# Pooling batch 0 in skewed steps, copying the transposed w1 once, and a new order of the main loop

## The chip, the cores and the metric

The kernel runs on one core of one Trainium2 chip. The time is that of one execution on the device in microseconds (us); the result compares medians of several executions. One further execution is recorded by the hardware profiler, and all lines of a profile come from that one. TensorE (PE) has a row for its matmuls and one for its weight loads (PEld, which overlap the matmuls); VectorE is DVE, ScalarE ACT, GpSimd POOL, SyncE SP.

## The reference

Two operations follow each other. The first is attention over a set of 32 inducing points, in both directions, on four batches of 12,544 tokens of 128 channels:

```python
scale = 1.0 / np.sqrt(C)
def mab(q, kv):
    s = scale * (q @ kv.transpose(0, 2, 1))
    s = s - s.max(-1, keepdims=True)
    a = np.exp(s)
    a /= a.sum(-1, keepdims=True) + 1e-09
    return a @ kv
h = mab(I, x)          # 32 pooled vectors per batch
y = mab(x, h)          # every token attends to the 32
```

The second is a maxout layer on the 50,176 rows of y, with 1,024 hidden units:

```python
g = np.maximum(y @ w1, y @ w2)
out = g @ w_out        # float32
```

## The kernel before

All matmuls run in float16. A chunk is 128 tokens; a batch has 98 chunks.

**Algebra.** The maximum is written as y w1 plus relu(y (w2 - w1)). As y is a mix of the 32 rows of h with the weights e, the kernel forms hwd = h (w2 - w1) and m1 = h (w1 w_out) once for each batch. A token's output is then relu(e hwd) w_out + e m1, divided by the sum of e at the end.

**Pooling of batch 0** stands ahead of everything else. x comes in eleven parts of 14 down to 3 chunks, loaded by POOL's queue; the first comes through SP and is cast on the chip. Each part is transposed on TensorE (`p1_transpose`; first half copied out by VectorE, second by ScalarE), gives scores against the inducing points, of which ScalarE takes the exponential (`p1_scores`), and is accumulated into h and the sums (`p1_accum`). A few matmuls on constant data (`fill`) keep TensorE busy in the first parts. Then h is scaled and copied (`small_h`), w1, which VectorE has negated in place, is transposed on TensorE into w1T (`weights_2`), the sums are turned into reciprocals rs and rw by VectorE (`small_sums`), and hwd comes in quarters and a half (`small_hwd`). w1T with w_out gives w1out (`weights_3`), which `small_m1` needs.

**The main loop** handles blocks of up to four quarters of up to four chunks. `stage` computes the scores of a block's tokens against h in four column tiles of the array; ScalarE takes the exponential into e2. A row phase (`phase`, the matmuls of L978) runs up to four jobs in four row tiles: a job is either 512 columns of e hwd, whose relu is taken by ScalarE (L994) or VectorE (L997), or the start of an output group with e m1. Final matmuls (L801) multiply relu by w_out into the group's bank; VectorE multiplies by the reciprocal of the sum of e (L828), and SP stores the result. Each of the eight PSUM banks is held by one job until ScalarE or VectorE has read it. `keep_busy` adds stopgap matmuls (L758) where a wait is foreseen.

**Pooling of batches 1 to 3** runs inside the main loop in six units of 16 chunks each: x is transposed by DMAs on SP's queue (L171, fourteen for a batch), `pool_scores` (L308) computes the scores of a unit in column tiles, ScalarE takes the exponential into one of five buffers eu (L319), SP transposes that by a DMA into eT (L345), and `pool_accum` (L364) accumulates two units at a time. Unit 5 takes over the buffer of unit 0. `small_rep`, `small_h`, `small_hwd` and `small_m1` follow.

**The order** is made while the kernel is built. A `Clock` adds up assumed durations for TensorE, ScalarE and VectorE and keeps for each bank the time at which it comes free. At each step the loop picks side work, a column job, a row phase or a final matmul by these times and by due dates counted in finished chunks (`at`). A pool score may be placed once the x transposes it needs were placed 8 us ago on that clock; for unit 5 it asks that the transpose of unit 0's exponential has been placed, not that it is over. The table `DEV` alters the choice at some steps: 1 prefers a final matmul, 2 a phase, 3 passes over column work, 4 allows it early. On the chip every engine then follows its own fixed list, waiting on semaphores.

Of the kernel before, what the change touches and what calls it, by code (L numbers as in the profile page):

```python
# [9 lines left out]
F16 = mybir.dt.float16  # L10
# [92 lines left out]
def kernel(  # L103
# [38 lines left out]
    def bank(shape, dtype=F32, only=None):  # L142
        i = min(range(8), key=lambda j: ck.bank[j]) if only is None else only
        uid[0] += 1
        return i, psum.tile(shape, dtype, name=f"ps{uid[0]}", tag=f"bank{i}", bufs=1)
# [51 lines left out]
    with tc.manual_schedule(engines={ET.PE, ET.DVE, ET.Activation, ET.Pool, ET.SP}):  # L197
# [63 lines left out]
        def p1_accum(b, i, lo=0, hi=P1):  # L261
            k0, n = parts[b][i]
            et, ready = st[b]["et", i]
            hi = min(hi, n)
            xn = xn_at[b, i]
            if b == 0:
                last = i == len(parts[0]) - 1
                ck.wait(ready, "p1")
                for j in range(lo, hi, 4):
                    m = min(4, hi - j)  # L270
                    nc.tensor.matmul(  # L271
                        out=st[0]["eps"][0 : m * M, 0:1],
                        lhsT=et[:, j : j + m, :].rearrange("p k m -> p (k m)"),
                        rhs=ones16[:, 0:1],
                        start=(i == 0 and j == 0),
                        stop=(last and j + m == n),
                        skip_group_check=True,
                    )
                for j in range(lo, hi):
                    nc.tensor.matmul(  # L280
                        out=st[0]["hps"][:, 0:M],
                        lhsT=xn[:, j, :],
                        rhs=et[:, j, :],
                        start=(i == 0 and j == 0),
                        stop=(last and j == n - 1),
                    )
                st[0]["end"] = ck.run(0.029 * (hi - lo) + 0.03 * ((hi - lo + 3) // 4))
                return
# [156 lines left out]
        def small_sums(es, ready):  # L445

            ps = st[0]["eps"]
            ck.wait(ready, "p1")
            nc.tensor.matmul(out=ps[:, 2:3], lhsT=rep32, rhs=es, start=True, stop=True, skip_group_check=True)
            end = ck.run(0.11)  # L450
            st[0]["rs"] = smp.tile([128, 1], F32, name="rs_0", tag="rs_")
            st[0]["rw"] = smp.tile([128, 1], F32, name="rw_0", tag="rw_")
            nc.vector.reciprocal(out=st[0]["rs"], in_=ps[:, 2:3])
            nc.vector.tensor_scalar(out=st[0]["rw"], in0=st[0]["rs"], scalar1=1.0 / scale, scalar2=None, op0=ALU.mult)
            ck.bank[st[0]["eb"]] = st[0]["rsr"] = ck.on_dve(end, 0.34)

        def small_hwd(b, halves=(0, 1)):
            if 0 in halves:
                st[b]["hwd"] = smp.tile([128, J], F16, name=f"hwd_{b}", tag="hwd")
            hwd = st[b]["hwd"]  # L460
            for half in halves:
                for n in range(2 if b == 0 and half == 0 else 1):
                    w = 256 if b == 0 and half == 0 else 512
                    bi, ps = bank([128, 512])
                    ps = ps[:, 0:w]
                    sl = slice(512 * half + w * n, 512 * half + w * (n + 1))
                    ck.wait(max(ck.bank[bi], st[b]["hT4r"]), "p1")
                    if b == 0:
                        nc.tensor.matmul(out=ps, lhsT=st[b]["hT4"], rhs=w2h[:, sl], start=True, stop=False)
                        nc.tensor.matmul(out=ps, lhsT=st[b]["hT4"], rhs=w1h[:, sl], start=False, stop=True)  # L470
                        end = ck.run(0.43 * w / 512)
                    else:
                        nc.tensor.matmul(out=ps, lhsT=st[b]["hT4"], rhs=w21[:, sl], start=True, stop=True)  # L473
                        end = ck.run(0.215)
                    if half == 0 and n == 0:
                        if b == 0:
                            nc.vector.tensor_scalar(
                                out=hwd[:, sl], in0=ps, scalar1=st[0]["rw"], scalar2=None, op0=ALU.mult
                            )
                        else:  # L480
                            nc.vector.tensor_copy(out=hwd[:, sl], in_=ps)
                        ck.bank[bi] = ck.on_dve(end, 0.07 + w / 970.0)
                    else:
                        nc.scalar.activation(
                            out=hwd[:, sl], in_=ps, func=AF.Copy, scale=st[0]["rw"] if b == 0 else 1.0
                        )
                        ck.bank[bi] = ck.on_act(end, 0.06 + w / 1200.0)
                    st[b]["hwdr"] = max(ck.bank[bi], st[b].get("hwdr", 0.0))
# [33 lines left out]
                nc.gpsimd.tensor_sub(w21[:, 512 * h : 512 * (h + 1)], w_of[h][0], w_of[h][1])  # L522

        def weights_2():
            for g in range(2):
                bi, ps = bank([128, 4, 128], F16)
                ck.wait(ck.bank[bi], "w")
                for j in range(4):
                    jb = 4 * g + j
                    nc.tensor.transpose(ps[:, j, :], w1h[:, 128 * jb : 128 * (jb + 1)], identity16)  # L530
                end = ck.run(0.056 * 4)
                if g == 0:
                    nc.vector.tensor_copy(out=w1T[:, 0:4, :], in_=ps)
                    ck.bank[bi] = ck.on_dve(end, 0.4)
                else:
                    nc.scalar.copy(out=w1T[:, 4:8, :], in_=ps)
                    ck.bank[bi] = w_of["w1T"] = ck.on_act(end, 0.5)

        def weights_3():
            bi, ps = bank([128, 512])  # L540
# [105 lines left out]
        def fill(n):  # L646
            bi, ps = bank([128, 512])
            for _ in range(n):
                nc.tensor.matmul(out=ps, lhsT=warm[:, 0:128], rhs=warm, start=True, stop=True)  # L649
            ck.run(0.22 * n)  # L650
# [7 lines left out]
        for n in ("h", "e"):  # L658
            st[0][n + "b"], st[0][n + "ps"] = bank([128, 512])
            ck.bank[st[0][n + "b"]] = INF  # L660
        for i in range(4):
            p1_transpose(0, i, 2 if i == 0 else 0)
            if i < 3:
                fill(2 - i // 2)
            if i == 0:
                bi, ps = bank([128, 512])
                nc.tensor.transpose(ps[:, 0:M], ind_sb, identity32[0:M, 0:M])
                nc.vector.tensor_copy(out=inducingT, in_=ps[:, 0:M])
                ck.bank[bi] = 0.0
                nc.vector.reduce_sum(out=diag, in_=identity32.rearrange("p (k m) -> p m k", m=M), axis=AX.X)  # L670
                for dst, f in ((rep32, DOWN / scale), (repd, 1.0)):
                    nc.vector.tensor_scalar(
                        out=dst.rearrange("p (k m) -> p k m", m=M),
                        in0=diag[:, None, :].broadcast_to((128, 4, M)),
                        scalar1=f,
                        scalar2=None,
                        op0=ALU.mult,
                    )
            if i > 0:
                p1_accum(0, i - 1)  # L680
            p1_scores(0, i)
        last = len(parts[0]) - 1
        p1_transpose(0, 4)
        p1_accum(0, 3)
        p1_transpose(0, 5)
        p1_scores(0, 4)
        for i in range(6, last + 1):
            p1_transpose(0, i)
            p1_scores(0, i - 1)
            p1_accum(0, i - 2)  # L690
        p1_scores(0, last)
        p1_accum(0, last - 1)
        p1_accum(0, last)
# [4 lines left out]
        sums = small_h(0)  # L698
        weights_2()
        small_sums(*sums)  # L700
        stage(blocks[0])
        small_hwd(0, (0,))
        blocks[0].staged = max(blocks[0].staged, st[0]["hwdr"])
# [174 lines left out]
        def want_linear():  # L878
# [12 lines left out]


        DEV = {
            31: 1, 54: 1, 107: 2, 141: 1, 148: 1, 177: 4, 201: 1, 231: 1, 268: 1, 285: 1, 289: 1, 297: 2,
            308: 3, 310: 4, 331: 1, 339: 4, 357: 4, 358: 4, 366: 1, 375: 1, 397: 1, 409: 1, 446: 3, 457: 1,
            463: 4, 465: 3, 488: 1, 518: 2, 542: 3, 567: 4, 612: 3, 653: 1, 752: 1, 805: 1, 810: 2, 829: 1,
            834: 4, 842: 1, 846: 1, 863: 1, 900: 1, 920: 4, 946: 1, 950: 1, 966: 1, 1005: 1, 1025: 1, 1050:
            2, 1111: 1, 1119: 1, 1138: 1, 1152: 1, 1163: 1, 1190: 1, 1201: 1, 1282: 1, 1294: 1, 1299: 1,
            1301: 4, 1349: 4, 1362: 3, 1363: 2, 1370: 4, 1379: 1, 1396: 2, 1435: 1, 1459: 1, 1469: 1, 1472:
            3, 1519: 1, 1534: 1, 1536: 3, 1543: 4, 1572: 3, 1606: 1, 1617: 4, 1635: 1, 1654: 3, 1686: 1,  # L900
            1701: 3, 1729: 1
        }
        LIMIT = -16

# [288 lines left out]
```

The softmax here doesn't subtract the row's maximum and nothing guards it: scores larger than these inputs give would overflow.

## Time and profile before

| what | value |
|---|---|
| median of 4 executions | 328.05 us (327.6 to 328.36) |
| the profiled execution | 327.6 us, of which its span 325.5 us |
| TensorE matmul, busy | 320.2 us, 98% |
| weight loads | 242.4 us, 74% |
| VectorE, busy | 282.4 us, 87% |
| ScalarE, busy | 281.8 us, 87% |
| GpSimd, busy | 25.4 us, 8% |
| final matmuls | 3,136 |
| relus on ScalarE and on VectorE | 465 of 605 ns, 319 of 682 ns |
| DMA | 53.65 MB, 165 GB/s in the mean |

The span runs from the first instruction of the program to the last; the profiled execution's time has some 2.1 us around it. A matmul's duration includes its way through the array, so the 220 ns of a final matmul are no measure of how fast they follow one another; starts are. A line of the timeline has start, length over all its instructions, engine, source line, operation, output and input, shape, count, and in brackets the idle time ahead of it with what ended it. In the list of waits and in the groups, an arrow names what an engine waited for.

### The profile page before, as it was taken

How to read it: one execution, taken by the hardware profiler on the slowest of the kernel's cores; microseconds unless marked ns; L12 is line 12 of the kernel's file. 1: busy time of each engine (PE TensorE's matmuls, PEld its weight loads, DVE VectorE, ACT ScalarE, POOL GpSimd, SP SyncE). 2: the span in 40 equal slices, each digit the busy share in tenths (PEclk: the TensorE clock that was granted, in tenths of full speed). 3: DMA queues.
4: the chain of work that ended last, by engine and by line, in shares of the span. 5: the costliest groups of instructions: out<-in, count | busy, mean ns of one | idle time of the engine just before them, and what ended most of it. 6: DMA issues, size and time to landing. Idle time of an engine off the chain costs nothing.

```text
span 325.5 us, 12587 instructions
## 1 busy us (share of the span) xinstructions
PE 320.2 (98%) x5404; PEld 242.4 (74%) x5404; DVE 282.4 (87%) x518; ACT 281.8 (87%) x564; POOL 25.4 (8%) x51
## 2 busy tenths in 40 slices
PE   7999999999999999999999999999999999999995
PEld 3886777777777777777777777777777777777785
DVE  3359998998989999999989989898999999989873
ACT  3689899999978999999988999899979999999961
POOL 7352030000040000000040000000000000000000
PEclk9999999999999999999999999999999999999999
DMA  8999999976299999984379999993422212222233
GB/s 206 207 206 214 286 240 191 193 203 141 99 182 244 193 271 198 196 169 130 101 141 240 222 250 185 191 200 105 135 96 99 83 66 101 99 99 99 89 112 112
DMA packets 70823, 53.65 MB, mean 165 GB/s; under 512 B 52176, under 2 KB 55408, under 8 KB 70768
## 3 DMA queue, kind: packets, MB, share of 16 engines
q1 hardware_dynamic: 64656, 38.63, 50.5%
q0 software_dynamic: 6112, 14.22, 22.4%
q8 instruction: 42, 0.69, 0.9%
q14 instruction: 13, 0.11, 0.1%
HBM read 28.33 MB, written 25.69 MB: 166 GB/s over the span
## 4 chain that ended last, share of the span: by engine, by line
PE 98%; ACT 0%; issue 0%; DVE 0%; ACTq 0%
PE ps L801 61%; PE ps L978 23%; PE ps L591 3%; PE ps L232 2%; PE ps L364 1%; PE ps L308 1%; PE ps L657 1%; PE ps L248 1%; PE ps L280 1%; PE ps L631 1%; PE ps L758 1%; PE ps L271 1%; PE ps L649 0%; PE ps L473 0%; PE ps L409 0%
## 5 line engine op out<-in xcount | busy, mean ns | idle before, releaser
L994 ACT ACTIVATE relu<-ps 128x512 f16<-128x512 f32 x465 | 245.4, 605 | 25.3 <-PE ps L978 16.2
L997 DVE TENSOR_SCALAR relu<-ps 128x512 f16<-128x512 f32 x319 | 204.9, 682 | 19.8 <-PE ps L978 18.3
L801 PE MATMUL ps<-woutp,relu 128*128 128x128 f16 x3136 | 217.9, 220 | 0.0
L801 PEld LDWEIGHTS <-relu 128*128 128x128 f16 x3136 | 177.0, 98 | 40.7 <-issue 30.2
L978 PE MATMUL ps<-e,hwd 32*128 32x512 f16 (+2 forms) x880 | 88.6, 360 | 0.0
L828 DVE TENSOR_TENSOR o<-ps,rp 128x512 f32<-128x512 f32 (+3 forms) x108 | 68.5, 634 | 5.7 <-PE ps L801 3.4
L978 PEld LDWEIGHTS <-hwd 32*128 32x128 f16 x880 | 24.5, 91 | 20.9 <-issue 0.8
L978 PE MATMUL ps<-m,e 32*128 32x128 f16 x381 | 38.8, 217 | 0.0
L978 PEld LDWEIGHTS <-e 32*128 32x128 f16 x381 | 21.3, 92 | 2.6
L165 POOL DMA_DIRECT2D xn<-in_x_dram x31 | 16.7, 551 | 8.1 <-DMA xn<-in_x_dram 4.4
L236 DVE COPY xT<-ps 128x512 f16<-128x512 f16 (+3 forms) x11 | 5.5, 504 | 7.8 <-PE ps L232 7.7
L603 ACT ACTIVATE e<-ps 128x512 f16<-128x512 f32 (+2 forms) x21 | 11.6, 570 | 0.0
L319 ACT ACTIVATE eu<-ps 128x512 f16<-128x512 f32 x18 | 10.8, 617 | 0.0
L591 PE MATMUL ps<-xT,hT 128*32 128x512 f16 (+3 forms) x114 | 10.1, 366 | 0.0
L164 POOL COPY pace<-hacc 128x1 f32<-128x1 f32 x2 | 0.4, 184 | 115.8 <-DVE hacc L397 115.8
L239 ACT COPY xT<-ps 128x768 f16<-128x768 f16 (+3 forms) x11 | 6.1, 556 | 2.8 <-PE ps L232 2.7
L232 PE MATMUL ps<-identity,xn 128*128 128x128 f16 x98 | 7.4, 218 | 0.1
L257 ACT ACTIVATE et<-ps 128x448 f16<-128x448 f32 (+4 forms) x11 | 4.5, 413 | 2.6 <-PE ps L248 2.6
L641 DVE RECIPROCAL rp<-ps 128x16 f32<-128x16 f32 (+2 forms) x28 | 6.7, 239 | 0.0
L232 PEld LDWEIGHTS <-xn 128*128 128x128 f16 x98 | 5.6, 97 | 1.3 <-DVE xn L653 0.9
L631 PE MATMUL ps<-ones_q,e 128*128 128x4 f16 x102 | 6.6, 165 | 0.0
L591 PEld LDWEIGHTS <-hT 128*32 128x32 f16 x114 | 2.6, 93 | 5.1 <-issue 4.2
(96 smaller groups left out, 112.2 us busy)
## 6 DMA issues: line engine op xcount, KB each, us to landing
out_dram<-o SPq DMA_DIRECT2D x90, 256.0 KB, 2.6
xn<-in_x_dram POOLq DMA_DIRECT2D x24, 448.0 KB, 12.1
out_dram<-o SPq DMA_DIRECT2D x10, 128.0 KB, 3.5
xn<-in_moe_w_dram POOLq DMA_DIRECT2D x4, 256.0 KB, 14.1
xn<-in_x_dram POOLq DMA_DIRECT2D x4, 224.0 KB, 10.1
xT<-xn SPq DMA_TRANSPOSE x42, 3.8
xf<-in_x_dram SPq DMA_DIRECT2D x1, 512.0 KB, 3.6
xf<-in_x_dram SPq DMA_DIRECT2D x1, 384.0 KB, 4.0
```

The costliest lines, as they stand in the source:

```text
L165: nc.gpsimd.dma_start(out=xn_at[b, i][:, 0:n, :], in_=xr[b, :, k0 : k0 + n, :])
L232: nc.tensor.transpose(ps[:, j, :], xn[:, g + j, :], identity16)
L319: nc.scalar.activation(out=eu, in_=ps, func=AF.Exp, scale=scale, accum_out=st[b]["es"][:, u : u + 1])
L591: nc.tensor.matmul(out=ps[32 * q : 32 * (q + 1), 128 * t : 128 * (t + n)], lhsT=hq, rhs=xT[:, c : c + n, :], start=True, stop=True, tile_p ...
L603: nc.scalar.activation(out=blk.e2[:, 0 : 128 * wd], in_=ps[:, 0 : 128 * wd], func=AF.Exp, scale=st[0]["rs"] if blk.b == 0 else scale,)
L631: nc.tensor.matmul(out=ps[:, 4 * t : 4 * t + 4], lhsT=blk.e2[:, 128 * t : 128 * (t + 1)], rhs=ones_q, start=True, stop=True,)
L641: nc.vector.reciprocal(out=blk.rp[:, 0:wd, :].rearrange("p t q -> p (t q)"), in_=ps[:, 0 : 4 * wd])
L801: nc.tensor.matmul(out=g.ps[:, 128 * c : 128 * (c + 1)], lhsT=g.blk.relu[q][:, 128 * (jb * w4 + t) : 128 * (jb * w4 + t + 1)], rhs=woutp[: ...
L828: nc.vector.tensor_mul(osb[:, 0:n, :], g.ps[:, 0 : n * C].rearrange("p (s c) -> p s c", s=n), rp)
L978: nc.tensor.matmul(**seq[i])
L994: nc.scalar.activation(out=dst, in_=src, func=AF.Relu)
L997: nc.vector.tensor_scalar(out=dst, in0=src, scalar1=0.0, scalar2=None, op0=ALU.max)
```

## The change

It has four parts.

1. Batch 0's parts go through one loop: transpose part i, scores of part i-1, accumulate part i-2. Before, the first four parts ran transpose, accumulate of the part before, scores of the same part, with a hand-written passage for parts 4 and 5; parts 6 to 10 already had the new form. The fillers keep their numbers (2, 2, 1), now ahead of the transposes of parts 1 to 3.
2. The eight transposes of w1 go into one bank instead of two, and VectorE copies all of it in one instruction (`weights_2b`), placed after the reciprocals. Before, VectorE and ScalarE copied one half each, VectorE ahead of the reciprocals.
3. The second half of batch 0's hwd (512 columns) is scaled and copied by VectorE instead of ScalarE. The first half stays as it was: 256 columns on each engine.
4. The table `DEV` is another one, so the loop's order differs in many places.

```diff
@@ small_hwd
-                    if half == 0 and n == 0:
+                    if half == 0 and n == 0 or b == 0 and half == 1:
@@ weights_2
-            for g in range(2):
-                bi, ps = bank([128, 4, 128], F16)
-                ck.wait(ck.bank[bi], "w")
-                for j in range(4):
-                    jb = 4 * g + j
-                    nc.tensor.transpose(ps[:, j, :], w1h[:, 128 * jb : 128 * (jb + 1)], identity16)
-                end = ck.run(0.056 * 4)
-                if g == 0:
-                    nc.vector.tensor_copy(out=w1T[:, 0:4, :], in_=ps)
-                    ck.bank[bi] = ck.on_dve(end, 0.4)
-                else:
-                    nc.scalar.copy(out=w1T[:, 4:8, :], in_=ps)
-                    ck.bank[bi] = w_of["w1T"] = ck.on_act(end, 0.5)
+            bi, ps = bank([128, NJB, 128], F16)
+            ck.wait(ck.bank[bi], "w")
+            for jb in range(NJB):
+                nc.tensor.transpose(ps[:, jb, :], w1h[:, 128 * jb : 128 * (jb + 1)], identity16)
+            w_of["turned"] = bi, ps, ck.run(0.056 * NJB)
+            ck.bank[bi] = INF
+
+        def weights_2b():
+            bi, ps, end = w_of["turned"]
+            nc.vector.tensor_copy(out=w1T, in_=ps)
+            ck.bank[bi] = w_of["w1T"] = ck.on_dve(end, 0.7)
@@ pooling of batch 0
-        for i in range(4):
+        last = len(parts[0]) - 1
+        for i in range(last + 1):
+            if i in (1, 2, 3):
+                fill(2 - i // 3)
             p1_transpose(0, i, 2 if i == 0 else 0)
-            if i < 3:
-                fill(2 - i // 2)
...
             if i > 0:
-                p1_accum(0, i - 1)
-            p1_scores(0, i)
-        last = len(parts[0]) - 1
-        p1_transpose(0, 4)
-        p1_accum(0, 3)
-        p1_transpose(0, 5)
-        p1_scores(0, 4)
-        for i in range(6, last + 1):
-            p1_transpose(0, i)
-            p1_scores(0, i - 1)
-            p1_accum(0, i - 2)
+                p1_scores(0, i - 1)
+            if i > 1:
+                p1_accum(0, i - 2)
         p1_scores(0, last)
         p1_accum(0, last - 1)
         p1_accum(0, last)
...
         weights_2()
         small_sums(*sums)
+        weights_2b()
         stage(blocks[0])
@@ the table of deviations (its first entries)
         DEV = {
-            31: 1, 54: 1, 107: 2, 141: 1, 148: 1, 177: 4, 201: 1, 231: 1, 268: 1, 285: 1, 289: 1, 297: 2,
+            0: 1, 15: 1, 24: 1, 40: 2, 89: 1, 100: 2, 132: 3, 164: 1, 200: 1, 296: 4, 298: 1, 316: 4, 343:
...
```

## The prediction

> **What bounds the kernel now.** I read the page first: engine shares, the chain that ended last, the costliest groups.
>
> ```profile
> PE 320.2 (98%) x5404; PEld 242.4 (74%) x5404; DVE 282.4 (87%) x518; ACT 281.8 (87%) x564; POOL 25.4 (8%) x51
> PE 98%; ACT 0%; issue 0%; DVE 0%; ACTq 0%
> L994 ACT ACTIVATE relu<-ps 128x512 f16<-128x512 f32 x465 | 245.4, 605 | 25.3 <-PE ps L978 16.2
> L997 DVE TENSOR_SCALAR relu<-ps 128x512 f16<-128x512 f32 x319 | 204.9, 682 | 19.8 <-PE ps L978 18.3
> L801 PE MATMUL ps<-woutp,relu 128*128 128x128 f16 x3136 | 217.9, 220 | 0.0
> ```
>
> The chain is TensorE alone. ScalarE (ACT) and VectorE (DVE) have 13% to spare and, by the waits, wait for TensorE. So the time is the matmul stream plus what makes it stop. I measured the stream in the timeline from start to start: a final matmul (L801) follows another by 0.056; from a final into a row phase (L978) 0.15 instead, from the phase's start to the next final 0.33, so a phase costs 0.42; a stage or pool-score group of four column matmuls takes 0.217, and 0.31 from the last one back to a final. After 36 us nothing exceeds these by more than about 0.2; between 24 and 36 the gaps beyond them sum to 1.0 us (0.37 in the phase at 24.65, 0.16 at 25.43, 0.19 at 32.21, 0.15 at 33.61, two of 0.07). TensorE stands still at the front or nowhere. Hence the timeline there:
>
> ```profile
> 19.81 0.33 PE L232 MATMUL ps<-identity,xn 128*128 128x128 f16 x3
> 20.65 0.43 DVE L697 TENSOR_SCALAR w1h<-w1h 128x1024 f16<-128x1024 f16 x1 [0.25 <-DMA w1h<-in_moe_w_dram]
> 21.43 0.61 PE L530 MATMUL ps<-identity,w1h 128*128 128x128 f16 x8
> 22.07 0.58 ACT L536 COPY w1T<-ps 128x512 f16<-128x512 f16 x1 [0.39 <-PE ps L530]
> 22.45 0.15 DVE L454 TENSOR_SCALAR rw<-rs 128x1 f32<-128x1 f32 x1
> 22.90 0.49 DVE L477 TENSOR_SCALAR hwd<-ps,rw 128x256 f16<-128x256 f32 x1 [0.30 <-PE ps L470]
> 23.17 1.06 ACT L484 ACTIVATE hwd<-ps,rw 128x256 f16<-128x256 f32 x2
> 24.13 0.68 ACT L603 ACTIVATE e<-ps,rs 128x512 f16<-128x512 f32 x1
> 24.27 2.51 DVE L997 TENSOR_SCALAR relu<-ps 128x512 f16<-128x512 f32 x4 [0.89 <-PE ps L978]
> 24.70 1.09 ACT L994 ACTIVATE relu<-ps 128x512 f16<-128x512 f32 x2
> ```
>
> To be seen: VectorE has a hole of 0.3 before its first hwd, and w1 lands only at 20.6 (issued 12.01, 8.6 to landing by its line). Then the stretch where batch 1 is pooled, for the new order moves its steps:
>
> ```profile
> 63.26 1.39 SPq L171 DMA_TRANSPOSE xT<-xn  x1
> 63.94 0.61 PE L308 MATMUL ps<-xT,inducingT 128*32 128x512 f16 x8
> 66.98 2.77 SPq L345 DMA_TRANSPOSE eT<-eu  x2
> 71.90 0.39 PE L308 MATMUL ps<-xT,inducingT 128*32 128x512 f16 x4
> 73.21 0.61 ACT L319 ACTIVATE eu<-ps 128x512 f16<-128x512 f32 x1
> ```
>
> The first line is batch 1's fourteenth x transpose; narrowed to it, the view says 4.3 to landing: 67.5. The third begins with eT of pool unit 0, 3.3 to landing: 70.3. The scores of unit 5 (71.90) need the one; its exponential (73.21) overwrites the buffer that the other reads (five eu buffers). Now both are in time.
>
> **The skill.** "PSUM — Partial Sum Buffer", Engine vs sequencer instructions: ScalarE and VectorE are strict FIFO and matmuls start in program order. The trace agrees: relus queue without overtaking (seven from 66.96). So one late operand stops all behind it. The same page, The four PSUM rules: eight 2 KiB banks; the transposed w1 (1,024 f16) fills one. "TensorE: Matmul & The Clock Gate", Wait — 56ns, not 53.3ns?: 55.6 and 215.7 ns for 128 and 512 columns; here 56 and 217. "DMA: Bandwidth & Descriptors", Latency and other measured facts: about 2 us fixed cost, growing with load. Here a transpose takes 3.0 to 3.8 (medians), up to 8.3 while the engines are full.
>
> **The change, part by part.**
>
> *Skewed steps.* Same matmuls, same 7 fillers; from part 6 on the order is the old one. Before, the accumulate of part 3 waits 0.47 for its exponential (15.20) and later transposes run 0.3 to 0.45 behind their landings; part 10 lands at 19.36 (issued 9.86, 9.5) and is transposed at 19.81. The new order removes that backlog, but w1's transposes cannot precede w1 scaled: 21.08 and a semaphore, 21.15, against 21.43. Gain at the first phase 0 to 0.26; I take 0.20.
>
> *w1T in one copy, half of hwd to VectorE.* ScalarE loses 0.58 and 0.69. VectorE, 0.20 earlier: rw done 22.40; copy of 1,024 columns 0.65 (the xT copy of that size lasts 0.69, overlaps a little), 23.05; first hwd 0.45, 23.50; second half: no row of VectorE has this form; 0.63 (the plain 512-column cast) to 0.75 (0.49 for 256 scaled columns plus 0.26 for 256 more); I take 0.70, 24.20. First VectorE relu 24.15, before 24.27. The copy is hidden only by the hole; without the 0.20 the first hwd would end at 23.70, 0.07 before the phase that needs it (23.77). ScalarE: e of block 1 waits for its stage matmuls (end 23.83, now 23.63), ends 24.37, before 24.81; first relu 24.3, before 24.70. The second phase's fourth job takes a bank that VectorE's first relu frees (24.95; matmul 25.02): now 24.83, so of 0.20 about 0.1 is left. The waits of 0.19 and 0.15 at 32.2 and 33.6 may shrink with an earlier ScalarE: 0.1. The 13 stopgap matmuls stay 13, 0.11 each: they cost the same whether needed or not. Front together: -0.2 (0 to -0.6).
>
> *The order found anew.* By the instruction order TensorE keeps 5,400 matmuls, 222 row phases and 33 column stretches; relus keep 465 to 319; POOL's queue, with all loads, is unchanged. One phase runs straight into a column stretch instead of via finals: 0.09+0.33-0.31, -0.1. The last 20 us are the same. What moves is batch 1's scores: before single, pair, pair, single (after 229, 313, 372, 455 finals), now single, triple, pair (230, 354, 405). SP's queue keeps its order through there: the transposes and eT keep their places, at 67.5 and 70.3, as SP issues without a pause from 61.9 to 69.7 (its own time, 1.2 to 1.4 a transpose).
>
> TensorE's time at the pair: the new final 354 starts near 61.2 (before 62.02, with 0.43 of scores and 0.4 of a column stretch not yet done); the phase brings the stage to 61.7, triple and return 62.7; then 51 finals 2.88, two phases 0.84 and one into column mode 0.41: 66.83. ScalarE: from 60.7 four relus at 0.55, e 0.65, three exponentials at 0.57 (59.66, 60.23, 60.80 in the trace): 65.26; six relus 68.56; exponential 4, 69.13.
>
> 1. ScalarE is so late after the triple that the phases near 64.1 and 65.3, and unit 4's scores (bank freed by the third relu, 66.95), each wait 0.05 to 0.15: +0.3 (0 to 0.6).
> 2. Unit 5's scores, due 67.2, wait for the transpose, 67.55: +0.35 (0 to 0.7). Behind them stands every later matmul.
> 3. Exponential 5 waits from 69.1 to 70.35 for eT 0. Behind it stand all ScalarE's relus; its bank is wanted by the phase due at 70.6 and comes at 71.0, and the next phase's last job is 0.15 late: +0.55 (0 to 1.2). ScalarE then catches up over some 10 us in which it has about 2 to spare.
>
> Against the front's -0.2 and the order's -0.1 stand +1.2: net +0.9. The profiled execution is 325.5 span in 327.6, the lowest of the four; so 328.5 for it, and with the median 328.05, 0.45 higher, **328.95**.
>
> **Rivals.** *The landings come in time* (0.28): SP's queue drains a microsecond earlier, or relus have more slack than I walked. For it: finals trail their relus by 2 us or more nearly everywhere, in both orders. Against it: SP is busy without a hole there, so nothing draws it forward. Then -0.3 and 0 to +0.6 of the three waits: 327.75 to 328.6, about 328.1, no change. This is also the case that the skew does nothing, as x's landings pace it.
>
> *ScalarE's relief at the front decides* (0.17), the other side: 0.4 us earlier on ScalarE removes most of the 1.0 us of waits between 24 and 36, and the three later waits stay under 0.3. Then -0.1-0.26-0.9+0.3: about 327.1. It decides only if eT 0 has landed by about 69.3.
>
> *The VectorE queue becomes the bound at the front*: the copy and the half in a row hold the first phase and delay relus. Counted above at +0.1 at most without the skew; it lies inside the forecast.
>
> **How the numbers follow.** Forecast 0.55: 328.95, alone 328.5 to 330.2 (all three waits high: -0.3+2.5). The range for 8 in 10 takes in no change and half of the faster case: 327.3 to 330.2. A measurement of this kernel tells about 0.2%, 0.66 us, from nothing. Forecast and rivals give slower 0.54, same 0.29, faster 0.17.
>
> **What would show it.** First phase near 23.57 and first ScalarE relu near 24.3: the front. A gap of 0.2 to 0.7 inside the pool scores near 67, and a ScalarE idle of about 1.2 before an eu exponential near 69 whose releaser is a DMA: the cluster. Wrong if ScalarE has no hole there, if eT 0 lands before 69.2, or if TensorE stops elsewhere, above all at batch 2's pooling near 138, where eT 1 has only about 1 us to spare.

## The result, and the profile after

The changed kernel takes 328.57 us (median of 33 executions, 327.95 to 329.92) against 327.93 us for the kernel before on the same chip (53 executions, 327.3 to 328.76): ratio 1.0022, 95% interval 1.0016 to 1.0027. It is 0.64 us slower. In a later comparison the ratio was 1.0026 (1.0017 to 1.0035).

The page of the changed kernel has nearly the same shares. First the busy times, then the chain of work by engine, then the relus of ScalarE and VectorE:

```profile
PE 320.9 (98%) x5404; PEld 242.9 (74%) x5404; DVE 282.7 (86%) x519; ACT 281.1 (86%) x562; POOL 25.5 (8%) x51
PE 96%; DMA 2%; ACT 1%; issue 0%; SPq 0%; DVE 0%; ACTq 0%
L985 ACT ACTIVATE relu<-ps 128x512 f16<-128x512 f32 x465 | 245.9, 603 | 26.7 <-PE ps L969 19.0
L988 DVE TENSOR_SCALAR relu<-ps 128x512 f16<-128x512 f32 x319 | 204.4, 681 | 18.4 <-PE ps L969 17.3
```

The chain now leaves TensorE at its beginning: 2% is the landing of the inducing points, for which TensorE waits before it transposes them (before, fillers stood ahead of that). Next the front:

```profile
16.74 0.87 PE L232 MATMUL ps<-identity,xn 128*128 128x128 f16 x7
20.19 0.33 PE L232 MATMUL ps<-identity,xn 128*128 128x128 f16 x3
20.79 0.43 DVE L688 TENSOR_SCALAR w1h<-w1h 128x1024 f16<-128x1024 f16 x1
21.81 0.61 PE L528 MATMUL ps<-identity,w1h 128*128 128x128 f16 x8
22.52 0.91 PE L589 MATMUL ps<-xT,hT 128*32 128x512 f16 x4
22.90 0.68 DVE L534 COPY w1T<-ps 128x1024 f16<-128x1024 f16 x1
24.44 0.75 DVE L477 TENSOR_SCALAR hwd<-ps,rw 128x512 f16<-128x512 f32 x1 [0.17 <-PE ps L470]
24.66 0.40 PE L969 MATMUL ps<-e,hwd 32*128 32x128 f16 x9
25.11 0.69 DVE L988 TENSOR_SCALAR relu<-ps 128x512 f16<-128x512 f32 x1
25.37 0.59 ACT L985 ACTIVATE relu<-ps 128x512 f16<-128x512 f32 x1
```

The first row phase starts at 24.66; the prediction had 23.57, and before it stood at 23.77:

```profile
23.77 0.40 PE L978 MATMUL ps<-e,hwd 32*128 32x128 f16 x9
```

Part 10 of x is transposed at 20.19 (before 19.81), w1 at 21.81 (21.43). Two groups are longer than their work: seven transposes take 0.87 where others of seven take 0.55, and the four stage matmuls at 22.52 take 0.91 where the same four take 0.40 before. The profile shows no semaphore that TensorE waits for in either; these two are called silent stops below. The third stretch is the pooling of batch 1:

```profile
66.98 2.53 SPq L345 DMA_TRANSPOSE eT<-eu  x2
67.81 0.62 PE L308 MATMUL ps<-xT,inducingT 128*32 128x512 f16 x8
69.36 0.62 ACT L319 ACTIVATE eu<-ps 128x512 f16<-128x512 f32 x1
69.93 0.62 ACT L319 ACTIVATE eu<-ps 128x512 f16<-128x512 f32 x1
```

The scores of units 4 and 5 run without a gap (eight matmuls in 0.62), and the two exponentials follow each other. The fourteenth x transpose was issued at 62.47 and landed at 65.47 (before 63.26 and 67.52); eT of unit 0 was issued at 66.98 as before, and landed at 69.71 (70.32). Both predicted holes are absent from this execution.

From the first row phase to the last matmul's end TensorE takes 298.91 us, before 298.52. So of the 1.37 us between the two profiled executions (328.97 and 327.6), 0.89 arises ahead of the first row phase, 0.39 behind it, and 0.1 outside. That split isn't that of the medians, which differ by 0.64; the experiments had to show why.

### The profile page after: what moved, and what is told of

It reads as the page before. It is cut to its first block, busy times and chain, and to the rows that moved or that the text cites. A ratio compares the mean times of both kernels' runs of the same rounds, so it can differ in the third digit from the quotient of the medians.

```text
span 326.8 us, 12575 instructions
## 1 busy us (share of the span) xinstructions
PE 320.9 (98%) x5404; PEld 242.9 (74%) x5404; DVE 282.7 (86%) x519; ACT 281.1 (86%) x562; POOL 25.5 (8%) x51
## 4 chain that ended last, share of the span: by engine, by line
PE 96%; DMA 2%; ACT 1%; issue 0%; SPq 0%; DVE 0%; ACTq 0%
PE ps L793 61%; PE ps L969 22%; PE ps L589 3%; DMA ind_sb<-in_inducing_dram 2%; PE ps L232 2%; PE ps L364 1%; PE ps L308 1%; PE ps L280 1%; PE ps L248 1%; PE ps L629 1%; PE ps L750 1%; PE ps L271 0%; PE ps L647 0%; PE ps L473 0%; PE ps L409 0%
## 5 line engine op out<-in xcount | busy, mean ns | idle before, releaser
L601 ACT ACTIVATE e<-ps,rs 128x512 f16<-128x512 f32 (+1 forms) x7 | 4.6, 661 | 1.7 <-PE ps L589 1.7
```

The source lines that it names most:

```text
L601: nc.scalar.activation(out=blk.e2[:, 0 : 128 * wd], in_=ps[:, 0 : 128 * wd], func=AF.Exp, scale=st[0]["rs"] if blk.b == 0 else scale,)
```

## The experiments

**Holding the order.** The planner's order depends on its clocks, so an edit at the front alone would change the loop too. In all experiments but the repeat of the changed kernel, the planner's clocks are set, behind the second row phase, to the values that they have there in the kernel before or in the changed one; the table `DEV` is of the same kernel. From the third row phase on, every engine's order is then exactly the old or the new one; the traces of all fourteen kernels agree with this for TensorE, ScalarE and VectorE.

```diff
         START = ck.pe
+        ck.pe, ck.act, ck.dve = 20.33866666666667, 21.785999999999998, 21.76866666666667
+        for j, t in zip(sorted(range(8), key=lambda j: ck.bank[j]), [20.325, ...]):
+            ck.bank[j] = t
+        blocks[0].staged, blocks[1].staged = 18.727999999999998, 19.848
...
```

### The parts one by one

Part 1 alone, on the order of before:

```diff
-        for i in range(4):
-            p1_transpose(0, i, 2 if i == 0 else 0)
...
+        for i in range(last + 1):
+            if i in (1, 2, 3):
+                fill(2 - i // 3)
+            p1_transpose(0, i, 2 if i == 0 else 0)
...
+            if i > 0:
+                p1_scores(0, i - 1)
+            if i > 1:
+                p1_accum(0, i - 2)
```

> The kernel before with part 1 alone (batch 0 in skewed steps); from the third row phase on, the order is that of before, held fixed. Prediction's theory (the skew gains a little, the pool cluster costs): first row phase 23.6 instead of 23.77, time 0 to 0.3 us below before. New theory (the skew sends scores and accumulate of parts 2 and 3 behind the transposes of part 4, and TensorE does not catch up with x until w1's transposes): transposes of part 5 are ready to go at their landing but part 6's start 0.3 late, w1's transposes near 21.8, first row phase 24.1 to 24.7, time 0.4 to 0.9 us above before. Third theory (the late first phase of the changed kernel is a stall of that one execution, not of its order): first phase within 0.15 of 23.77, time within 0.2.

Measured: 328.10 us, ratio to before 1.0002 (0.9994 to 1.0011). In its profile the first row phase is at 24.57, 0.80 later than in the profile of before, and TensorE stays 0.78 to 0.81 late to the end; yet the medians differ by 0.1.

Parts 2 and 3 alone:

```diff
-                    if half == 0 and n == 0:
+                    if half == 0 and n == 0 or b == 0 and half == 1:
...
-                for j in range(4):
...
+            for jb in range(NJB):
...
+            nc.vector.tensor_copy(out=w1T, in_=ps)
...
+        weights_2b()
```

> The kernel before with parts 2 and 3 alone (w1T copied once behind the reciprocals, second half of hwd by VectorE); order from the third row phase on held as in before. Prediction's theory: first VectorE relu about 0.2 later than 24.27 because the copy is not hidden without the skew, first ScalarE relu about 0.2 earlier than 24.70, hwd's first quarter ends 23.70 and the first phase stays at 23.77; time within 0.2 us of before. New theory: the same, 0 to -0.3. If the copy and the half on VectorE are themselves what holds the first phase: first phase 24.0 or later, time 0.3 us or more above before.

Measured: 327.83 us, 0.9996 (0.9987 to 1.0004). First row phase 23.98.

Part 4 alone, the old front with the new table and its order:

```diff
         DEV = {
-            31: 1, 54: 1, 107: 2, 141: 1, 148: 1, 177: 4, 201: 1, 231: 1, 268: 1, 285: 1, 289: 1, 297: 2,
+            0: 1, 15: 1, 24: 1, 40: 2, 89: 1, 100: 2, 132: 3, 164: 1, 200: 1, 296: 4, 298: 1, 316: 4, 343:
...
```

> The kernel before with part 4 alone: old front, and from the third row phase on exactly the order of the changed kernel. Prediction's theory: unit 5's scores wait near 67 for an x transpose (0.2 to 0.7), ScalarE stands 0.8 to 1.4 before an eu exponential near 68 for eT of unit 0; time 0.7 to 1.2 us above before, more than the changed kernel's 0.64. New theory (the front decides, the cluster meets its data): no such wait, time -0.1 to +0.4 us against before.

Measured: 328.31 us, 1.0009 (1.0000 to 1.0018). Unit 5's scores run at 67.48, its x transpose had landed at 64.76; the two exponentials stand at 68.80 and 69.37, and eT of unit 0 landed at 69.16. No hole, but 0.2 to spare.

The changed kernel with part 1 undone, so parts 2 to 4:

```diff
-        for i in range(last + 1):
...
+        for i in range(4):
...
+        p1_transpose(0, 4)
+        p1_accum(0, 3)
+        p1_transpose(0, 5)
+        p1_scores(0, 4)
```

> The changed kernel with part 1 undone (old steps of batch 0), its order from the third row phase on held fixed. Prediction's theory: undoing the skew costs 0 to 0.3, so 0.6 to 0.9 us above before. New theory: first row phase back near 23.8, 0.4 to 0.9 us faster than the changed kernel, so -0.3 to +0.3 us against before.

Measured: 328.65 us, 1.0020 (1.0013 to 1.0027). Undoing the skew gains nothing. The expectation that the front carried the 0.9 fell here.

The changed kernel with part 4 undone, so parts 1 to 3 on the old order (the diff of part 4 turned round):

> The changed kernel with part 4 undone: its front, and from the third row phase on exactly the order of before. If the new order is what costs (0.3 alone, 0.8 on top of the copies by the runs so far): 327.8 to 328.1, 0.5 to 0.8 us under the changed kernel. If the skewed front costs the 0.8 to 0.9 us that its profile shows: 328.6 or more, as the changed kernel. Main loop as in the run of the copies alone, end of the stream less first row phase 298.4.

Measured: 328.05 us, 1.0003 (0.9995 to 1.0011). The old order takes back most of the loss.

What follows, each effect taken in three surroundings: the new order costs 0.0009, 0.0024 and 0.0019 of the time, in the mean 0.0017 or 0.6 us; the skew 0.0002, 0.0007 and 0.0002, 0.1 us; the copies -0.0004, 0.0001 and 0.0011, 0.1 us. Single differences are uncertain by about 0.001, so only the order's is told from nothing. TensorE's time from the first row phase to the end says the same with less scatter: 298.39 to 298.52 in all seven profiles on the old order, 298.64 to 299.41 in all seven on the new one.

### Why a front that is 0.8 later in the profile costs 0.1

In the four profiles with the old steps the first row phase starts 17.49 us after the second half of x part 0 is transposed, to 0.01: 6.28 to 23.77, 6.49 to 23.98, 6.50 to 23.98, 7.24 to 24.73. TensorE runs through this stretch as one rigid chain: each delay of its start goes on unchanged. The start depends by up to 0.2 on when x lands (the first transpose stands between 5.18 and 5.35 in the fourteen profiles), and by more on when TensorE reaches full speed. The start in the kernel before, and with part 1 undone:

```profile
5.18 0.62 PE L232 MATMUL ps<-identity,xn 128*128 128x128 f16 x8
5.63 0.59 PE L649 MATMUL ps<-warm 128*128 128x512 f16 x2
6.28 0.49 PE L232 MATMUL ps<-identity,xn 128*128 128x128 f16 x6
```

```profile
5.29 1.04 PE L232 MATMUL ps<-identity,xn 128*128 128x128 f16 x8
6.12 1.06 PE L647 MATMUL ps<-warm 128*128 128x512 f16 x2
7.24 0.33 PE L232 MATMUL ps<-identity,xn 128*128 128x128 f16 x3
```

Eight transposes and two fillers take 0.45 and 0.65 in the one, 0.83 and 1.12 in the other: there TensorE is still at half speed (a transpose follows another by 0.107 instead of 0.056). The skewed steps hand less of this on, as they take the inducing points directly behind part 0. In the changed kernel these landed at 7.15 and were transposed at 7.29, 0.82 behind the second half (6.47); with part 1 alone the second half came at 6.87, and they were transposed at 7.30 without a wait. So the start that was 0.40 earlier gained nothing.

The second half of part 0 is reached at 6.28 in the profile of before, the earliest of all fourteen (up to 7.24, the middle at 6.5): that profile is a lucky start. With the skew the first row phase lies between 24.05 and 24.79 in seven profiles, 24.4 in the mean, with the old steps between 23.77 and 24.73 in four, 24.1 in the mean. This brings the 0.8 down to 0.3. The medians say 0.1, uncertain by about 0.2; with so few profiles the two agree, but more is not shown.

### What holds the skewed front

The two silent stops lie behind matmul 223 and matmul 351 of the program, 128 matmuls and their 128 weight loads apart. Of the seven profiles of the skewed steps with their five fillers, all show the second and four the first; the old steps show neither. In the trace TensorE's instructions come by DMA in packets of 16,384 bytes, 42 of them, which makes one for each 256 of its 10,808 matmuls and weight loads. From the list of DMA queues of the changed kernel between 14.7 and 14.9, with packets, MB and share of 16 engines:

```profile
q8 instruction: 1, 0.02, 30.4%
```

One such packet starts in this window of 0.2 us, and one in the window from 20.65. The packet records put the starts of the two fetches at 14.86 and 20.81, and TensorE goes on at 17.10 and 23.03, 2.24 and 2.22 later. In these seven profiles and the four with the old steps, TensorE reaches one of the two places 22 times. The eleven times that it came 1.7 to 2.11 us after the fetch began, it stopped, and went on 2.2 to 2.45 after it; the eleven times that it came 2.19 or later, it lost 0.01 at most. Before, the fetches begin at 13.62 and 19.87, and TensorE reaches the places 2.79 and 2.27 later, at 16.41 and 22.14. The Trainium skill ("Runtime: NRT & Kernel Launch", Instruction fetch mechanics) says that the sequencer fetches blocks of 16 KiB, 256 instructions, by its own DMA queue while it runs, and that the cost is mostly hidden. The trace agrees on the block; hidden it is not where TensorE runs through small matmuls without a wait.

Then the fillers. They stand on TensorE's path in the skewed steps, ahead of parts 1 to 3:

```diff
-            if i in (1, 2, 3):
-                fill(2 - i // 3)
+            if i == 2:
+                fill(2)
```

> The skewed steps of part 1 with the order of before, and the fillers cut from 2, 2, 1 to 0, 2, 0: they stand on TensorE's path in the skewed steps. If they and the two silent stops (at matmul 223 and 351 of the program, where a fetch of instructions began 2.2 us earlier) are what holds the skewed front: parts 3 to 6 transposed 0.4 earlier, first row phase 23.5 to 24.0 instead of 24.6, time 0.3 to 0.7 us below the skew alone (328.1). If the landings of x pace it: first phase within 0.2 of 24.6, time within 0.2 of the skew alone. If TensorE's clock falls in the gaps left: transposes of part 2 or 3 at 0.1 each instead of 0.056, time 0.3 us above.

Measured: 327.74 us, 1.0002 (0.9993 to 1.0010; one of its 14 executions took 329.16). First row phase 23.73. The four stage matmuls take 0.40 again: with three matmuls fewer ahead, the second boundary falls three matmuls later in the work, behind the last of the four. TensorE stands still there, and goes on at 22.43, 2.42 after its fetch began (20.01) and 0.41 after the stage matmuls; without a stop that step takes 0.33 (22.14 to 22.47 before). So the stop has moved with the count of instructions and shrunk to 0.08. But the first row phase of one profile is again earlier than the median bears out: the ratio is that of part 1 alone (1.0002), so the expected gain of 0.3 to 0.7 us did not come.

The same with parts 2 and 3:

> The run with fewer fillers together with parts 2 and 3 of the change, order of before: the parts that looked best. If the gains add: 0.15 under the run with fewer fillers alone, 0.4 to 0.9 us under before (327.1 to 327.6). If the one copy of w1T and the half of hwd on VectorE become the path once TensorE is earlier: no gain over the run with fewer fillers alone, first hwd waits for VectorE.

Measured: 327.55 us, 0.9991 (0.9983 to 0.9999), all 13 executions between 327.26 and 327.75. It is 0.3 us faster than before and scatters half as much; the same parts with five fillers had 1.0003. Its profile still has a stop, larger here, in the timeline and in the list of waits of line L469 (us, times):

```profile
21.89 0.40 PE L589 MATMUL ps<-xT,hT 128*32 128x512 f16 x4
22.67 0.28 PE L469 MATMUL ps<-w2h,hT 128*128 128x256 f16 x1 [0.38 <-PE ps L589]
```

```profile
  DMA w2h<-in_moe_w_dram: 0.7, 1
```

The list puts the wait down to w2. But w2 landed at 22.26, 0.41 before TensorE went on. At the 36 other places in the fourteen profiles where the view names a DMA that TensorE waited for (the stop of the run before this one aside), TensorE went on 0.14 after the landing at the latest, mostly 0.04; so w2 would have held it to 22.40 at most. In the profile of before the same step has no stop:

```profile
22.14 0.40 PE L591 MATMUL ps<-xT,hT 128*32 128x512 f16 x4
22.47 0.28 PE L469 MATMUL ps<-w2h,hT 128*128 128x256 f16 x1
```

The place is the boundary behind matmul 351 again. Its fetch began at 20.21, and TensorE goes on 2.46 later, as at the other stops. So the fetch is the likelier cause of the stop of 0.44 (0.77 against 0.33).

The last experiment was made on the reading that w2 paces the front, and puts the w1 products, which do not need it, ahead of those with w2:

```diff
+                for n in range(2):
+                    nc.tensor.matmul(
+                        out=ps[:, 0:256], lhsT=st[0]["hT4"], rhs=w1h[:, 256 * n : 256 * (n + 1)], start=True, stop=False
+                    )
...
-                        nc.tensor.matmul(out=ps, lhsT=st[b]["hT4"], rhs=w2h[:, sl], start=True, stop=False)
-                        nc.tensor.matmul(out=ps, lhsT=st[b]["hT4"], rhs=w1h[:, sl], start=False, stop=True)
+                        if first:
+                            nc.tensor.matmul(out=ps, lhsT=st[b]["hT4"], rhs=w1h[:, sl], start=True, stop=False)
+                        nc.tensor.matmul(out=ps, lhsT=st[b]["hT4"], rhs=w2h[:, sl], start=False, stop=True)
```

> The fastest kernel so far (skewed steps with fewer fillers, the copies of parts 2 and 3, the order of before), and the two quarters of hwd start with w1, which has landed, before w2, for which TensorE waits near 22.3. If w2's landing paces the front: second quarter 0.2 earlier after the landing, first row phase 0.15 to 0.25 earlier relative to it, time 0.4 to 0.6 us under before. If VectorE's copy of w1T holds the first quarter instead: no gain over the run without it (0.3 under before).

Measured: 327.63 us, 0.9989 (0.9983 to 0.9996). The median is that of the run without it, so a gain is below what can be told. In the profile the first row phase moved from 23.98 to 23.79, though w2 landed 0.09 later:

```profile
22.49 0.39 PE L466 MATMUL ps<-w1h,hT 128*128 128x256 f16 x2
```

Both readings have room for this: these products do not need w2, and their fetch, begun at 20.22, let TensorE go on 2.27 later instead of 2.46, which is the same 0.19. So this run does not tell them apart; the lags after w2's landing do.

### Whether the predicted waits occur at all

The changed kernel once more:

> The changed kernel itself once more, to stand beside the next two on the same chip and to show whether the two silent stops of TensorE in its front come back. 0.5 to 0.8 us above before. Fetch theory: a stop inside the four stage matmuls at matmul 351, ending 2.2 to 2.5 us after the fetch of instructions near 20.8 began; the one at matmul 223 only if it is reached less than that after its fetch. Chance theory: no stop at these two places.

Measured: 328.77 us, 1.0026 (1.0017 to 1.0035). The stop at 351 is there (0.24), the one at 223 is not: its fetch began at 13.90 and TensorE reached it at 16.30. And this execution shows the prediction's third wait:

```profile
66.82 2.53 SPq L345 DMA_TRANSPOSE eT<-eu  x2
68.76 0.62 ACT L319 ACTIVATE eu<-ps 128x512 f16<-128x512 f32 x1
69.97 0.60 ACT L319 ACTIVATE eu<-ps 128x512 f16<-128x512 f32 x1 [0.51 <-PE ps L330]
70.52 0.57 PE L969 MATMUL ps<-e,hwd 32*128 32x512 f16 x4
```

eT of unit 0 landed at 69.88 here, 3.1 after its issue, and ScalarE's exponential of unit 5 begins 0.09 later, after 0.51 of idleness (the view names the last semaphore of TensorE, which had come long before). The row phase at 70.52 is drawn out to 0.57, and TensorE is 0.21 later behind it than in the first profile, 0.04 of it from the scores of unit 5.

To see what this wait is worth without the profiler, the exponential of unit 5 gets a buffer of its own:

```diff
-            eu = etp.tile([128, 512], F16, name=f"eu_{b}_{u}", tag="eu", bufs=NEU)
+            if (b, u) == (1, 5):
+                eu = w1T[:, 0:4, :].rearrange("p j t -> p (j t)")
+            else:
+                eu = etp.tile([128, 512], F16, name=f"eu_{b}_{u}", tag="eu", bufs=NEU)
```

> The changed kernel, but the exponential of unit 5 of batch 1 has a buffer of its own (that of w1T, free by then), so it cannot wait for the transpose of unit 0; same order on every engine. Prediction's theory (its third wait, 0.55): 0.3 to 0.6 us under the changed kernel's 328.57, and fewer executions above 329. New theory (the transpose lands 0.2 to 0.3 before it is wanted): 0 to 0.15 us.

> The run with a buffer of its own for the exponential of unit 5, once more, since its first ratio (1.0012) lay between the two theories. Prediction's theory (executions without the profiler do meet its third wait): 0.25 to 0.5 us under the changed kernel beside it. New theory: within 0.15 of it.

Measured: 328.26 us, 1.0012 (1.0004 to 1.0020), and 328.27 us, 1.0011 (1.0003 to 1.0020) beside the changed kernel's 1.0022 and 1.0026. The buffer takes back 0.0010 and 0.0015, in the mean 0.4 us, and of executions above 329.1 there are none of 26, where the changed kernel has seven of 49. But not all of it need be this wait. In the three profiles of kernels with the new order, the copies and five buffers, one row phase stops for 0.25:

```profile
154.25 1.09 ACT L985 ACTIVATE relu<-ps 128x512 f16<-128x512 f32 x2 [0.27 <-PE ps L969]
155.13 0.63 PE L969 MATMUL ps<-e,hwd 32*128 32x512 f16 x4
```

ScalarE begins that relu 0.25 after the last semaphore that it can need, so its bank is late for the phase. In the profiles with the extra buffer, and in that of the order alone, the relu begins at once. Why is open. One hint: where this relu stops, it is the 320th of ScalarE's instructions in the trace (those of its sequencer counted), and where it does not, the 319th or 322nd; and in all three a packet of a second queue of instructions, of 8,192 bytes, starts 0.9 after it. So a boundary in ScalarE's own instructions may be the cause, and the extra buffer would then remove the stop by changing the count. No run tests this. The third wait is worth between 0.1 and 0.4 us in the mean, depending on how much of the buffer's gain is this stop.

With the extra buffer, and batch 1's x transposes three chunks earlier in SP's queue (a further edit keeps the planner's times for them, so that the other engines' order stays):

```diff
-            t_first, t_step = (6, 2.2) if b == 1 else (-6, 3.4)
+            t_first, t_step = (3, 2.2) if b == 1 else (-6, 3.4)
```

> As the run beside it, and batch 1's x transposes stand three finished chunks earlier in SP's queue (about 2.5 us); the order on TensorE, ScalarE and VectorE is that of the changed kernel. If unit 5's scores or any earlier scores of batch 1 meet a late landing in executions without the profiler (the prediction's second wait): 0.2 to 0.5 us under the run beside it. If not: within 0.15 of it. If the earlier transposes hold up output stores behind them on SP's queue: slower by 0.2 or more.

Measured: 328.37 us, 1.0014 (1.0008 to 1.0021), no better than the run beside it. The earlier issue bought nothing at the end of the queue: the fourteenth transpose was issued at 63.71, later than in the changed kernel, and landed at 68.13. So its profile shows the second predicted wait:

```profile
67.21 0.62 PE L309 MATMUL ps<-xT,inducingT 128*32 128x512 f16 x6
68.17 0.39 PE L309 MATMUL ps<-xT,inducingT 128*32 128x512 f16 x2 [0.35 <-DMA xT<-xn]
```

Inside unit 5's scores TensorE stops, and everything behind is 0.73 later. In the changed kernel's own two profiles that transpose landed 2.6 before it was wanted, and just when it was wanted (67.44, where these matmuls were put off by 0.04).

## Why the prediction was right and wrong

The time, 328.57, lies 0.4 under the forecast, and the new order's cluster in batch 1 is part of the loss, as forecast. But that the sum came out was in part luck, by errors that offset each other.

- **The skew, -0.20: wrong.** It is +0.1 (not told from zero), and 24.66 stands where 23.57 was predicted. The step that failed is "the new order removes that backlog". The wait of 0.47 before part 3's accumulate is gone, but the scores of part 3 and the accumulate of part 2, 32 matmuls that the old steps had done by then, now stand behind part 4's transposes and take 0.99 (14.56 to 15.55, by the starts); later steps of seven chunks take 0.8, about as much as the landings are apart, so the backlog never goes. Nor did it count that the fillers lie on the path, or the fetch of instructions, for which the wait of 0.47 had left time. And the profile it was measured against was a lucky start.
- **The copies: about right.** w1T's copy takes 0.68 (taken as 0.65), the half of hwd 0.75 (0.70, with 0.75 as the upper bound). The first ScalarE relu comes 0.71 after the first row phase instead of 0.93, predicted 0.73. The waits at the two row phases near 33 did not shrink (0.19 and 0.15 as before). Alone on the old order, the second row phase begins 0.88 after the first, as before. Its third job starts 0.2 earlier, its fourth only 0.05, and over the whole loop 0.1 is left (298.39 against 298.52). In the median that cannot be told.
- **The order's fewer mode changes, -0.1: right in the net.** With the order alone, the ways into and out of column groups sum to 0.31 less by the starts (15.62 against 15.93), and the steps inside them to 0.19 more, 0.08 of it in the triple.
- **ScalarE late after the triple, +0.3: too large.** The extra time inside the triple's scores is 0.08, and a final at 72.89 is held for 0.08.
- **Unit 5's scores wait for x, +0.35: not in the changed kernel.** The step that failed is "the transposes and eT keep their places, at 67.5 and 70.3": SP's queue kept its order, not its times. The transpose went out 0.8 earlier and took 3.0 instead of 4.3. The place came from one profile, and these times spread: in the seven profiles on the old order the transpose goes out between 62.18 and 63.26. The rival "the landings come in time" had this right (its upper end, 328.6, comes to 328.35 by its own terms, 328.05 - 0.3 + 0.6). The wait itself is real where the landing is late: 0.73, at the upper end of the range named, with the transposes moved, and 0.04 in the changed kernel's second profile.
- **The exponential waits for eT 0, +0.55: right in kind, too large.** It is absent from one profile and costs TensorE 0.17 in the other; in the median it is worth 0.1 to 0.4. The step that was mis-sized is the landing of eT, assumed 3.3 after its issue. It took 2.7 and 3.1, so the exponential waited not at all and 0.6 (by the starts), where 1.2 was walked.
- **What was not seen.** For batch 2 the sums' replication on TensorE waits for VectorE, which takes the accumulate out behind two relus:

```profile
165.79 0.29 DVE L397 TENSOR_TENSOR hacc<-ps,hacc 128x129 f32<-128x129 f32 x1
166.24 0.46 PE L409 MATMUL ps<-hacc,repd 128*128 128x129 f32 x2 [0.16 <-DVE hacc L397]
```

  Over the three batches the ways into that matmul and the next of its kind (into `small_h`) take 0.19 more than before. Where neither the stop at 155 nor a wait near 69 shows, the new order costs 0.24 to 0.29 (298.64 and 298.69 against 298.40 with the copies, 298.77 against 298.50 without): this 0.19, 0.10 in finals and 0.07 in row phases, and a net of -0.12 from the column groups above. Add 0.25 at 155 and 0.1 or so for the third wait, and the sum is 0.6, as the medians have it. The last two are read from a few profiles, so the agreement is an account and not a proof.

The forecast's net of the front, -0.2, was 0.4 too low, and that of the order, +1.1, was 0.5 too high.

## What to carry to other kernels

A stretch where one engine runs as a rigid chain hands every delay of its start to the end, so one profile of it says little of a median: lay several profiles over each other from a common point before judging 0.1 or 0.8 us there. Moving a step behind another removes its wait only if the work between fits into the gaps of the inputs; count that work, the fillers among it, against the spacing of the landings. A wait is put down to the semaphore that the view can see: if the landing lies 0.4 us before the start, look for another cause. And an order that leaves a DMA 0.2 to 0.6 us of room can pay for it in some executions even if one profile shows no wait: a further buffer is worth a try there.

## What the runs showed of the hardware

- At the two boundaries of 256 instructions in the front, TensorE stopped for 0.1 to 0.8 us whenever it got there 1.7 to 2.11 us after the fetch of the next block began, and lost 0.01 us at most when it got there 2.19 us or more after it (22 cases). The fetch began 31 to 68 matmuls ahead of its need there; in the loops of the kernel before and the changed one it began 71 to 138 ahead, where matmuls follow each other less closely.
- Matmuls begin at half speed (0.43 for 512 columns, from 1.19 on), and full speed (0.22) came between about 4 and 7 us from the start, in programs that are equal up to there: within the first nine such matmuls in four of the fourteen profiles, only with the eleventh or behind it in two. The Trainium skill ("TensorE: Matmul & The Clock Gate", What's actually happening) says that the clock is released after about 3.4 us of sustained work, by a window that runs freely, so that the moment varies by some 0.5 us from run to run. The trace agrees that the moment varies; the spread here is about 3 us.
- One transpose by DMA, the fourteenth of batch 1, at the same place of the queue took 3.0 us from issue to landing in one execution of the changed kernel and 4.8 in another.
